# The second MLP of a mixer kernel: 768 tokens by slabs, then two blocks of 768 whose first layer takes Strassen's seven products

## The chip, the cores and the metric

The kernel runs on one core of a Trainium2 chip. The metric is the device time of one execution in microseconds. A core has TensorE (matmuls into PSUM, eight banks of 128 x 2 KB), VectorE, ScalarE and GpSimd, each with its own instruction queue worked in order, SBUF as working memory, and DMA engines that the queues of SyncE (SP) and GpSimd (POOL) start here.

## The reference

Three stages follow one another; the change is in the last. `x` there is 4 x 576 tokens of 512 values, so 2304 tokens, 18 tiles of 128.

```python
X = np.fft.fft(x, axis=1); X = np.fft.fft(X, axis=2)
u = x + np.real(X)
un = (u - mean(u)) / sqrt(var(u) + 1e-06)          # over the 512 values
out = u + np.maximum(un @ w_ch1, 0.0) @ w_ch2      # 512x2048, 2048x512
```

Ahead of it stand random-feature attention and a first mixer MLP (tokens, then channels 512-1536-512). The second MLP's weights come as float64 and are used to more than fp32r's precision: a value is split into a high and a low part, and each product is high x high + high x low + low x high, three matmuls.

## The kernel before, in words

All matmuls of the MLPs are fp32r, 128 x 128 weights against up to 512 columns. `widen` (line 253) turns a 1 MB slab of 64-bit weights on VectorE (seven steps) and ScalarE (one) into high and low parts in the buffers `stg`, `cvy`, `cvo` (two of each, pool `cv`), and `slab` (line 334) stores it to HBM as `kept`; that is done in the background of the attention and of the first MLP.

The **second MLP** has 16 slabs of 128 hidden units, and walks the tokens in five blocks: four of 512, one of 256 (lines 1164 to 1171). For each block and slab `up` (line 689) does 12 matmuls (4 slices of the input x 3 products) into a PSUM bank `H`; `relu` (line 776) lets ScalarE write the high part `hh` and VectorE the low part `hl`; `down` (line 1124) adds 3 products for each token tile into four banks `A`, one per tile. `mlp` (line 783) runs `up` of a slab ahead of `down` of the slab before, so TensorE always has a slab's work between a bank's last matmul and its reader. Blocks go through the slabs forwards and backwards in turn (`turns`), and `refill` (line 644) loads slabs from `kept` on SP's queue into up to nine 1 MB buffers (`wa`, `wb`, and the four of `cv` once widening is over), evicting what is used latest, so a part of the slabs stays from one block to the next.

Between the matmuls stands **side work**, a list with a cost for each item in us. `Side.step(budget)` (line 207) is called once per slab, adds the budget to a credit of at most 4.0, and emits items of `lead` as long as the credit pays for them; a `None` in the list ends the step. Instructions are emitted in this order on each engine (`manual_schedule`). `dft(b)` (line 862) makes the spectrum of one batch entry (VectorE sums `even0` to `odd3`, matmuls `stage1e`, `stage1o`, `stage2`, VectorE again in `plus`, `minus`, `nat`), `norm(c)` (line 1069) the statistics and `un`, the normalized rows of block c. `ff_split` (line 1111) turns `un` by TensorE transposes (bank `S`, two of them) into the operand `u`, high and low parts, at the end of the block before.

PSUM: two banks `H`, four `A`, two `S`. The lines that the prediction's steps touch are those named here, and in the trace line 696 is the first layer's matmul, 1132 the second layer's, 779 and 780 the two halves of the relu, 665 the load of a slab, 1116 the transposes.

Of the kernel before, what the change touches and what calls it, by code (L numbers as in the profile page):

```python
# [9 lines left out]
F32 = mybir.dt.float32  # L10
F32R = mybir.dt.float32r
I32 = mybir.dt.int32
# [23 lines left out]
SLOT0_US, SLOT1_US, SLOT_US, FIRST_US, SHORT_US, CH_US, FF_US, SAVED_US = 1.2, 0.45, 1.2, 3.9, 1.2, 3.7, 3.7, 4.0  # L36
# [77 lines left out]
def layout(q, k, v, omega, moe_w_tok1, moe_w_tok2, moe_w_ch1, moe_w_ch2, moe2_w_ch1, moe2_w_ch2):  # L114
# [26 lines left out]
    def slabs(a, b, n):  # L141
        a = a[COL].reshape(4, 128, n, 128).transpose(2, 1, 0, 3).reshape(n, 128, 512)
        b = b[:, COL].reshape(n, 128, 512)
        return words(np.concatenate([a, b], axis=2))

# [8 lines left out]
        "wch": slabs(moe_w_ch1, moe_w_ch2, NCH),  # L154
        "wff": slabs(moe2_w_ch1, moe2_w_ch2, NFF),
# [79 lines left out]

@with_exitstack
def mix_kernel(ctx: ExitStack, tc: tile.TileContext, qt, kt, va, om, w1, w2, wch, wff, t1, t2, out):
# [15 lines left out]
    def widen(src, n, done):  # L253
# [54 lines left out]

        f = n / 1024
        return (load, lambda: (done(st), busy.remove(k))), [  # L310
# [23 lines left out]
    def slab(ff, j):  # L334
        def store(st):
            kept[ff, j] = dram.tile([128, 2, 1024], F32, name="kept")
            side.queue.dma_start(out=kept[ff, j], in_=st["o"].bitcast(F32))
            whole.add((ff, j))
        return widen((wff if ff else wch)[j].bitcast(I32), 1024, store)
# [195 lines left out]
    def tok_weights():  # L535
# [17 lines left out]
        def chunk(w, lo, n, done):  # L553
            return widen(w.bitcast(I32)[:, 2 * lo:2 * lo + 2 * n], n, lambda st: done(st, lo))
# [63 lines left out]
    mlp0 = {}  # L618

    def enter_mlp():  # L620

        pl.close()
        for name, n in (("ub", 1), ("wa", 1)):
            mlp0[name] = ctx.enter_context(tc.tile_pool(name=name, bufs=n, reuse_waits="tile"))
        u = mlp0["u"] = operand()
        slots.extend((mlp0["wa"], f"wa{i}") for i in range(2))

        def begin():
            mlp0["hb"] = up(weights(*seq[0]), *u, ch_cols(0))

        early.extend([refill] + [lambda k=k: ch_split(0, u, [k]) for k in range(4)])
        early.extend([refill, begin])
# [5 lines left out]
    seq = [(False, j) for c in range(NBLK) for j in turns(NCH, c)]  # L638
    seq += [(True, j) for c in range(B + 1) for j in turns(NFF, c)]
    slots = []  # L640
    here = {}
    at = [0]

    def refill(need=None):

        if (True, NFF - 1) in whole and len(here) + len(slots) < 8:
            slots.extend((cv, tag) for tag in ("stg0", "stg1", "cvo0", "cvo1"))
        for q in range(at[0], len(seq)):
            s = seq[q]
            if s in here:  # L650
                continue
            if s == need:
                side.until(lambda: s in whole)
            if s not in whole:
                return
            if slots:
                slot = slots.pop(0)
            else:
                after = {h: seq.index(h, at[0]) if h in seq[at[0]:] else len(seq) for h in here}
                h = max(after, key=after.get)  # L660
                if after[h] <= q:
                    return
                slot = here.pop(h)[0]
            t = slot[0].tile([128, 2, 1024], F32R, tag=slot[1], name="w")
            sync.dma_start(out=t.bitcast(F32), in_=kept[s])
            here[s] = slot, t

    def weights(ff, j):
        if (ff, j) not in here:
            refill((ff, j))  # L670
        return here[ff, j][1]
# [17 lines left out]
    def up(wt, uh, ul, n):  # L689

        hi, lo = halves(wt, 0)
        hb = bank("H")
        c = 0
        for kk in range(4):
            for a, u in ((hi, uh), (hi, ul), (lo, uh)):
# [497 lines left out]
```

## Time and profile before

| | us |
|---|---|
| three runs | 964.81, 966.81, 967.01 |
| median | 966.81 |
| span of the profiled execution (first to last instruction) | 962.7 |
| TensorE busy | 944.0 (98%) |
| VectorE busy | 556.3 (58%) |
| ScalarE busy | 273.2 (28%) |
| GpSimd busy | 106.9 (11%) |

The profile is of one execution, which has no time of its own in the list of runs: its span is 4.1 us under their median. Times in rows are us from the span's start unless marked ns. Matmuls are pipelined, so a matmul's own duration overlaps its neighbour's; what one costs is read from the starts of many.

### The profile page before, as it was taken

To read this page: it belongs to the slowest core of one execution; us is meant where nothing else is said; L and a number is where in the kernel's file an instruction comes from. 1 tells how busy PE (TensorE), PEld (TensorE's weight loads), DVE (VectorE), ACT (ScalarE), POOL (GpSimd) and SP (SyncE) were. 2 spreads that over 40 slices of the span, in tenths; PEclk is the share of its full clock that TensorE was granted. 3 is DMA by queue.
4 is the path that set the end of the run, shared out by engine and by line. 5 is a ranking of instruction groups with operands and counts; after the bars stand their busy time and mean duration, and the time that the engine had idled before them with its cause. 6 is when DMAs were issued, how large, how long until landed. Compare 5 with 4: busy or idle time off the path is not lost.

```text
span 962.7 us, 13202 instructions
## 1 busy us (share of the span) xinstructions
PE 944.0 (98%) x5248; PEld 820.6 (85%) x5248; DVE 556.3 (58%) x1100; ACT 273.2 (28%) x613; POOL 106.9 (11%) x102
## 2 busy tenths in 40 slices
PE   7999998999999999999999999999999999999998
PEld 7999898888889988888888888888888888888897
DVE  5997989986776777766767532154345434411211
ACT  5876765742122212211312111111111111210111
POOL 3443333321110011000000000000000000000000
PEclk9999999999999999999999999999999999999999
DMA  8764454388898495373376672034103410351080
GB/s 269 232 201 163 148 215 180 126 307 321 344 392 334 158 353 182 146 251 126 132 262 219 225 305 82 0 131 176 44 1 131 175 45 1 115 191 44 24 324 25
DMA packets 33261, 170.80 MB, mean 177 GB/s; under 512 B 3632, under 2 KB 4272, under 8 KB 15664
## 3 DMA queue, kind: packets, MB, share of 16 engines
q1 hardware_dynamic: 27152, 126.78, 36.9%
q0 software_dynamic: 5904, 43.06, 11.8%
q8 instruction: 41, 0.67, 0.3%
q14 instruction: 20, 0.16, 0.1%
q10 hardware_dynamic: 144, 0.13, 0.0%
HBM read 132.08 MB, written 34.08 MB: 173 GB/s over the span
## 4 chain that ended last, share of the span: by engine, by line
PE 88%; DVE 10%; ACT 1%; issue 1%; DMA 0%; DVEq 0%; ACTq 0%
PE H L696 36%; PE A L1132 20%; PE A L819 15%; PE A L413 3%; PE A L574 2%; PE H L447 2%; DVE mx L427 2%; PE N L489 2%; PE S L997 1%; DVE cvo L298 1%; DVE x L505 1%; PE S L1010 1%; PE S L587 1%; PE S L1116 1%; DVE cvo L306 1%; PE S L574 1%
## 5 line engine op out<-in xcount | busy, mean ns | idle before, releaser
L696 PE MATMUL H<-uh,w 128*128 128x512 f32 (+1 forms) x1120 | 341.0, 371 | 1.5 <-ACT x L528 1.5
L780 DVE SCALAR_TENSOR_TENSOR hl<-H,hh 128x512 fp32r<-128x512 f32 (+1 forms) x140 | 89.2, 637 | 257.5 <-ACT hh L779 257.1
L696 PEld LDWEIGHTS H<-uh,w 128*128 128x128 f32 x1120 | 205.0, 189 | 36.5 <-ACT x L528 1.7
L779 ACT ACTIVATE hh<-H 128x512 fp32r<-128x512 f32 (+1 forms) x140 | 77.8, 555 | 506.3 <-PE H L696 504.1
L696 PE MATMUL H<-ul,w 128*128 128x512 f32 (+1 forms) x560 | 206.3, 368 | 0.0
L1132 PE MATMUL A<-w,hh 128*128 128x512 f32 x576 | 146.9, 391 | 0.0
L1132 PEld LDWEIGHTS A<-w,hh 128*128 128x128 f32 x576 | 106.6, 188 | 21.0
L696 PEld LDWEIGHTS H<-ul,w 128*128 128x128 f32 x560 | 105.6, 189 | 16.7
L819 PE MATMUL A<-hh,w 128*128 128x512 f32 (+1 forms) x480 | 108.7, 369 | 0.0
L819 PEld LDWEIGHTS A<-hh,w 128*128 128x128 f32 x480 | 84.2, 188 | 15.0
L1132 PE MATMUL A<-w,hl 128*128 128x512 f32 x288 | 80.6, 390 | 0.0
L431 ACT ACTIVATE f<-A,mx 128x128 f32<-128x128 f32 x200 | 57.5, 388 | 29.6 <-DVE mx L427 25.3
L1132 PEld LDWEIGHTS A<-w,hl 128*128 128x128 f32 x288 | 54.1, 188 | 11.4
L819 PE MATMUL A<-hl,w 128*128 128x512 f32 (+1 forms) x240 | 59.2, 368 | 0.0
L427 DVE TENSOR_REDUCE mx<-A 128x4 f32<-128x512 f32 x71 | 48.3, 682 | 4.3 <-PE A L413 2.9
L819 PEld LDWEIGHTS A<-hl,w 128*128 128x128 f32 x240 | 42.6, 188 | 7.6
L298 DVE SCALAR_TENSOR_TENSOR cvo<-cvo,stg 128x1024 f32<-128x1024 int32 (+2 forms) x32 | 41.0, 1283 | 0.0
L447 PE MATMUL H<-v,f 128*128 128x65 f32 x320 | 40.0, 270 | 0.0
L447 PEld LDWEIGHTS H<-v,f 128*128 128x128 f32 x320 | 39.1, 192 | 0.2 <-DVE kvs L452 0.2
L294 DVE SCALAR_TENSOR_TENSOR cvo<-cvy,cvo 128x1024 int32<-128x1024 int32 (+2 forms) x32 | 38.6, 1207 | 0.4
L306 DVE SCALAR_TENSOR_TENSOR cvo<-cvo,cvy 128x1024 fp32r<-128x1024 f32 (+2 forms) x32 | 38.8, 1212 | 0.0
L282 ACT ACTIVATE cvy<-cvy 128x1024 f32<-128x1024 f32 (+2 forms) x32 | 32.6, 1019 | 14.3 <-DVE cvy L275 14.3
(187 smaller groups left out, 1185.6 us busy)
## 6 DMA issues: line engine op xcount, KB each, us to landing
w<-kept SPq DMA_DIRECT2D x80, 1024.0 KB, 5.1
kept<-cvo POOLq DMA_DIRECT2D x21, 1024.0 KB, 6.3
stg<-in_wff_dram POOLq DMA_DIRECT2D x16, 1024.0 KB, 6.1
stg<-in_wch_dram SPq DMA_DIRECT2D x9, 1024.0 KB, 6.2
kept<-cvo SPq DMA_DIRECT2D x7, 1024.0 KB, 5.2
v<-in_va_dram SPq DMA_DIRECT2D x20, 260.0 KB, 4.0
ks<-in_kt_dram SPq DMA_DIRECT2D x18, 256.0 KB, 3.7
qs<-in_qt_dram SPq DMA_DIRECT2D x18, 256.0 KB, 2.7
```

The costliest lines, as they stand in the source:

```text
L282: act.mul(out=st["y"], in_=st["y"], mul=2.0 ** -112)
L294: dve.scalar_tensor_tensor(out=st["h"], in0=st["y"].bitcast(I32), scalar=-0x80000000, in1=st["h"], op0=ALU.bitwise_and, op1=ALU.bitwise_or)
L298: dve.scalar_tensor_tensor(out=st["l"].bitcast(F32), in0=st["l"], scalar=2.0 ** 32, in1=st["lw"].bitcast(U32), op0=ALU.mult, op1=ALU.add)
L306: dve.scalar_tensor_tensor(out=st["o"][:, 1, 0:n], in0=st["l"].bitcast(F32), scalar=2.0 ** -52, in1=st["y"], op0=ALU.mult, op1=ALU.mult)
L427: dve.tensor_reduce(out=mx, in_=p4, axis=AX.X, op=ALU.max, negate=True)
L431: act.activation(out=f[:, hh], in_=p4[:, hh], func=AF.Exp, bias=mx[:, hh])
L447: pe.matmul(out=kvp[b, g][:, hh * 65:hh * 65 + 65], lhsT=ft["k", i, g][:, hh, :], rhs=src["v", i, int(off > 0)][:, 4 * g + hh, :], start=( ...
L696: pe.matmul(out=hb[:, 0:n], lhsT=a[:, kk * 128:kk * 128 + 128], rhs=u[:, kk, 0:n], start=(c == 0), stop=(c == 11))
L779: act.activation(out=hh, in_=hb[:, 0:n], func=AF.Relu)
L780: dve.scalar_tensor_tensor(out=hl, in0=hb[:, 0:n], scalar=0.0, in1=hh, op0=ALU.max, op1=ALU.subtract)
L819: pe.matmul(out=acc[i][:, 0:cols], lhsT=a[:, cs], rhs=v, start=(j == 0 and c_ == 0), stop=(j == NCH - 1 and c_ == 2))
L1132: pe.matmul(out=acc[t], lhsT=a[:, t * 128:t * 128 + 128], rhs=w, start=(j == 0 and c_ == 0), stop=(j == NFF - 1 and c_ == 2))
```

## The change

The 18 token tiles are divided anew (`ROWS`). Tiles 0 to 3 (512 tokens) and 4 to 5 (256) keep the old way, slab by slab, as blocks 0 and 1. Tiles 6 to 11 and 12 to 17 are two *paired blocks* of 768 tokens each. There the 16 slabs are taken as 8 pairs of 256 hidden units; the first layer of a pair is a product of a 2 x 2 matrix of weight quarters (128 hidden units x 256 inputs each) with a 2 x 2 matrix of operand quarters (256 inputs x 384 tokens), and takes seven products (Winograd's form of Strassen's method: P1 to P7) where eight would be the plain way. Each product is 6 matmuls of 384 columns (2 slices x 3 products of parts). The sums that join products are done on VectorE (`u2`, `vv`, `held`, `c21`) from banks `X` and `Y`, the two `H` banks.

A paired block goes in two passes (`paired_block`). In the first, per pair, the seven products give hidden values of all 768 tokens; those of the first 384 tokens go through the relu and, one pair later, through the second layer (18 matmuls, `todo`, spread between the products in lots of 4, 5, 4 and 5); those of the other 384 wait unrectified in `held`. The second pass does the second layer of `held`, slab by slab backwards, 9 matmuls a slab, while the next block's operands are made (`prepare_ff`).

The four sums of weight quarters (P3, P5, P6, P7) are made once per pair: `sum_pair` on GpSimd (one sum of 1024 columns, four of 256, and the low part of 1024), with a copy on ScalarE, in blocks 0 and 1, and are stored to HBM beside the quarters. The sums of operand quarters are made with the transposes: for the first paired block partly in block 1 (`prepare_early`) and, for P3, P7 and P4, inside its first pair (`prepare_late`), which turns 18 of the 24 tiles again; for the second in the first's second pass.

Weights of the paired blocks are loaded in pieces of 512 KB (two products' quarters, or a slab's second layer) into six buffers (`ffw`); nothing is kept from one block to the next. Blocks 0 and 1 have six buffers of 1 MB (`wd` is new, those of `cv` are gone). `refill` has become a class `Slots` with the same rule of eviction; the last two slabs are bound to three of the buffers. Steps of side work come twice per slab in blocks 0 and 1, at 1.3 and 0.65, and four times a pair in the paired blocks, at 1.5; CH_US goes from 3.7 to 4.0.

```diff
-SLOT0_US, SLOT1_US, SLOT_US, FIRST_US, SHORT_US, CH_US, FF_US, SAVED_US = 1.2, 0.45, 1.2, 3.9, 1.2, 3.7, 3.7, 4.0
+SLOT0_US, SLOT1_US, SLOT_US, FIRST_US, SHORT_US, CH_US, FF_US, S_US, SAVED_US = 1.2, 0.45, 1.2, 3.9, 1.2, 4.0, 2.6, 1.5, 4.0
+NP = NFF // 2
+HALF = 384
+RT = HALF // 128
+PLAIN = [range(0, 4), range(4, 6)]
+PAIRED = [range(6, 12), range(12, 18)]
+ROWS = PLAIN + PAIRED
+P1, P2, P4, P6, P3, P7, P5 = 0, 1, 3, 4, 5, 6, 7
+PIECES = [(P1, P6), (P2, P5), (P3, P7), (P4,)]
...
+    def keep(queue, to, t):
+        for a in range(2):
+            queue.dma_start(out=to[:, :, a], in_=t.bitcast(F32)[:, a].rearrange("p (c n) -> p c n", c=4))
+    def first(p):
+        def store(st, free):
+            kept[1, p] = dram.tile([128, 8, 2, 256], F32, name="kept1")
+            keep(side.queue, kept[1, p][:, 0:4], st["o"])
+            whole.add((1, p))
+            free()
+        return widen(wff[2 * p].bitcast(I32), 1024, store)
...
+    mix.allow = lambda q, slot: q < len(mix.seq) - 2 or slot[1] in ("wa0", "wa1", "wd")
...
+    def sum_pair(p):
+        k = p % 2
+        w = mix.get((1, p))
+        y = cv.tile([128, 1024], F32, tag=f"cvy{k}", name="cvy")
+        v = y.rearrange("p (c n) -> p c n", c=4)
+        pool.tensor_tensor(out=v, in0=w[:, :, 0], in1=w[:, :, 1], op=ALU.add)
+        pool.tensor_tensor(out=v[:, 3], in0=v[:, 2], in1=v[:, 3], op=ALU.add)
+        pool.tensor_tensor(out=v[:, 2], in0=v[:, 0], in1=v[:, 2], op=ALU.subtract)
+        pool.tensor_tensor(out=v[:, 0], in0=v[:, 3], in1=v[:, 0], op=ALU.subtract)
+        pool.tensor_tensor(out=v[:, 1], in0=v[:, 1], in1=v[:, 0], op=ALU.subtract)
+        so = cv.tile([128, 2, 1024], F32R, tag=f"cvo{k}", name="so")
+        def high():
+            act.copy(out=so[:, 0], in_=y)
+            side.later(low, 1)
+        def low():
+            pool.tensor_tensor(out=so[:, 1], in0=y, in1=so[:, 0], op=ALU.subtract)
+            side.later(store, 3)
+        def store():
+            keep(sync, kept[1, p][:, 4:8], so)
+            whole.add((3, p))
+        side.later(high, 4)
...
+            if c == 0 and n % 2 and n < NFF - 1:
+                sum_pair(x[0])
...
+    def prepare_late(q):
+        xa, xb, t2 = held[NP - 1][:, 0], held[NP - 1][:, 1], temps()[2 + q]
+        def b12():
+            act.copy(out=xb, in_=turned(0, q, 1))
+        def b22():
+            pb = turned(0, q + 2, 1)
+            dve.tensor_tensor(out=xb, in0=pb, in1=xb, op=ALU.subtract)
+            parts_of(P3, q, pb)
+        def b21():
+            pb = turned(0, q + 2, 0)
+            dve.tensor_tensor(out=xa, in0=pb, in1=t2, op=ALU.subtract)
+            parts_of(P7, q, xb)
+            parts_of(P4, q, xa)
+        return [b12, b22, b21]
...
-    for c in range(B + 1):
-        if c in (1, 2):
-            side.lead += dft(1 + c)
-        if c < B:
-            side.lead += norm(c + 1)
-        v = operand() if c < B else None
-        ff_block(c, u, ff_prepare(c + 1, v) if c < B else [], FF_US)
-        u = v
+    side.lead += norm(1) + dft(2)
+    v = operand()
+    ff_block(0, u, ff_prepare(1, v), FF_US)()
+    side.lead += norm(2) + [None, (0.0, begin_ff)] + prepare_early(0) + prepare_early(1)
+    put = ff_block(1, v, [], FF_US / 2)
...
+    side.drain()
+    pm.close()
+    fp = ctx.enter_context(tc.tile_pool(name="fp", bufs=1, reuse_waits="tile"))
+    ff = {}
+    flow = []
+    due = []
...
+    def fetch_ff(x, pl_, tag):
+        k, p_, i = x
+        if k == 2:
+            t = pl_.tile([128, 2, 512], F32R, tag=tag, name="w2t")
+            sync.dma_start(out=t.bitcast(F32), in_=kept[2, p_][:, :, i * 512:i * 512 + 512])
+            return t
+        ids = PIECES[i]
+        t = pl_.tile([128, 2, 2, 256], F32R, tag=tag, name="w1t")
+        step = ids[1] - ids[0] if len(ids) > 1 else 1
+        sync.dma_start(out=t[:, 0:len(ids)].bitcast(F32), in_=kept[1, p_][:, ids[0]:ids[-1] + 1:step])
+        return t
...
+    def product(to, w, i, start):
+        uh, ul = operands(i)
+        n = 0
+        for q in range(2):
+            cs = slice(q * 128, q * 128 + 128)
+            for a, v in ((0, uh), (0, ul), (1, uh)):
+                pe.matmul(out=to, lhsT=w[:, a, cs], rhs=v[:, q], start=(start and n == 0), stop=(n == 5),
+                          skip_group_check=True)
+                n += 1
...
+    def paired_block(c, todo, uses, after):
+        s1, u2, vv, c21 = temps()
+        acc = [None] * RT
+        def pace():
+            if c or p_:
+                side.step(S_US)
+        for p_ in range(NP):
+            X, Y = (bank("H")[:, 0:HALF] for _ in range(2))
+            h = hbuf[4 * (p_ % 2):4 * (p_ % 2) + 4]
+            w = ffw.get((1, p_, 0))
+            product(X, w[:, 0], P1, True)
+            act.copy(out=s1, in_=X)
+            product(Y, w[:, 1], P6, True)
+            dve.tensor_tensor(out=u2, in0=Y, in1=s1, op=ALU.add)
+            ffw.used()
+            pace()
+            run(todo, 4)
+            w = ffw.get((1, p_, 1))
+            product(X, w[:, 0], P2, False)
+            relu_parts(h[0:2], X)
+            product(Y, w[:, 1], P5, True)
+            dve.tensor_tensor(out=vv, in0=Y, in1=u2, op=ALU.add)
+            pace()
+            run(todo, 5)
+            ffw.used(1 + uses)
+            w = ffw.get((1, p_, 2))
+            product(Y, w[:, 0], P3, False)
+            dve.tensor_tensor(out=held[p_][:, 0], in0=Y, in1=u2, op=ALU.add)
+            product(X, w[:, 1], P7, True)
+            dve.tensor_tensor(out=held[p_][:, 1], in0=X, in1=vv, op=ALU.add)
+            ffw.used()
+            pace()
+            run(todo, 4)
+            w = ffw.get((1, p_, 3))
+            product(X, w[:, 0], P4, False)
+            dve.tensor_tensor(out=c21, in0=X, in1=u2, op=ALU.add)
+            relu_parts(h[2:4], c21)
+            pace()
+            run(todo)
+            ffw.used(1 + uses)
+            if after:
+                after()
+            after, uses = None, 1
+            if p_ == 0:
+                acc = [bank("A") for _ in range(RT)]
+            for s_ in range(2):
+                todo += downs(acc, h[2 * s_:2 * s_ + 2], (2, p_, s_), p_ + s_ == 0, p_ + s_ == NP)
...
+        for n, x in enumerate(slabs):
+            if n == 1 and steps:
+                side.until(lambda: (len(PLAIN) + c + 1, 2 * RT - 1) in uns, side.lead)
+            if n and steps:
+                steps.pop(0)()
+            if n + 2 < len(slabs):
+                hs[n + 2] = part(n + 2)
+            mats = downs(acc, hs.pop(n), (2, *x), n == 0, n == len(slabs) - 1)
+            if n < len(slabs) - 2:
+                run(mats)
+                ffw.used()
+                side.step(S_US)
+            else:
+                left += mats
+        return left, 1, lambda: finish(c, 1, acc)
...
+    carry = prepare_late(0) + prepare_late(1), 0, None
+    for c in range(len(PAIRED)):
+        if c == 0:
+            side.lead += dft(3) + norm(3)
+        carry = paired_block(c, *carry)
+    run(carry[0])
+    ffw.used(2)
+    carry[2]()
```

## Rows read from the trace of the kernel before

**Rows 1.** The page: busy time of engines (1), chain that ended last by engine (4).

```profile
PE 944.0 (98%) x5248; PEld 820.6 (85%) x5248; DVE 556.3 (58%) x1100; ACT 273.2 (28%) x613; POOL 106.9 (11%) x102
...
PE 88%; DVE 10%; ACT 1%; issue 1%; DMA 0%; DVEq 0%; ACTq 0%
```

**Rows 2.** Windows: stretch, length, busy time by engine, granted clock, DMA share, GB/s.

```profile
0.00:100.00 100.00, 92.70 (x740) 89.58 (x740) 78.61 (x163) 71.37 (x194) 38.82 (x36) 1.00 0.67 217
...
700.00:800.00 100.00, 100.00 (x492) 84.41 (x491) 45.01 (x106) 15.53 (x31) 0.00 (x0) 1.00 0.23 85
```

**Rows 3.** Chain in order of time, end of the fourth and start of the fifth block.

```profile
901.63 2.72 PE A L1132 x12
904.35 2.72 PE H L696 x12
907.51 2.75 PE A L1132 x12
...
917.70 1.43 PE H L696 x12
```

**Rows 4.** Timeline of TensorE, matmuls of 288 columns: six from the first row on.

```profile
211.12 0.42 PE L587 MATMUL S<-w2hl,h1h 128*128 128x288 f32 x2
...
211.91 0.39 PE L696 MATMUL H<-uh,w 128*128 128x512 f32 x1
```

**Rows 5.** Groups by line and shape, pieces of 384 columns: busy, mean ns | idle.

```profile
L686 DVE TENSOR_TENSOR ul<-x,uh 128x384 fp32r<-128x384 f32 x4 | 2.2, 554 | 0.0
...
L685 ACT CAST uh<-x 128x384 fp32r<-128x384 f32 x4 | 2.1, 513 | 0.0
```

**Rows 6.** Timeline of one slab: last matmul of its first layer, then the relu.

```profile
605.14 0.39 PE L696 MATMUL H<-uh,w 128*128 128x512 f32 x1
...
605.57 0.60 ACT L779 ACTIVATE hh<-H 128x512 fp32r<-128x512 f32 x1 [4.84 <-PE H L696]
606.20 0.69 DVE L780 SCALAR_TENSOR_TENSOR hl<-H,hh 128x512 fp32r<-128x512 f32 x1 [4.75 <-ACT hh L779]
```

**Rows 7.** Timeline of VectorE: newton and un; even1 and even2 of a dft.

```profile
481.25 0.17 DVE L1092 RECIPROCAL y<-y 128x4 f32<-128x4 f32 x1
...
482.24 1.92 DVE L1101 TENSOR_SCALAR un<-U,mv,y 128x512 f32<-128x512 f32 x4
...
732.77 0.44 DVE L886 TENSOR_TENSOR sp<-fo 1x289 f32<-1x289 f32 x1
...
734.55 0.67 DVE L780 SCALAR_TENSOR_TENSOR hl<-H,hh 128x512 fp32r<-128x512 f32 x1
735.16 0.44 DVE L893 TENSOR_TENSOR fv<-fo 128x289 f32<-128x289 f32 x1
...
736.48 0.61 DVE L904 TENSOR_TENSOR fo<-fv 128x432 f32<-128x432 f32 x1
```

**Rows 8.** Groups by line and shape: GpSimd's subtractions, VectorE's at 640 columns.

```profile
L516 POOL TENSOR_TENSOR xl<-x,xh 128x512 fp32r<-128x512 f32 x18 | 28.3, 1570 | 29.7 <-ACT xh L515 25.9 <-issue 3.8
...
L401 POOL TENSOR_TENSOR kl<-ks,kh 128x512 fp32r<-128x512 f32 x17 | 22.9, 1349 | 80.9 <-ACT kh L400 63.9 <-PE H L447 8.3 <-DVE kh L398 5.2
...
L298 DVE SCALAR_TENSOR_TENSOR cvo<-cvo,stg 128x640 f32<-128x640 int32 x2 | 1.6, 814 | 0.0
```

**Rows 9.** Timeline of VectorE and GpSimd side by side.

```profile
47.42 1.29 POOL L401 TENSOR_TENSOR kl<-ks,kh 128x512 fp32r<-128x512 f32 x1 [2.55 <-ACT kh L400]
47.80 1.53 DVE L298 SCALAR_TENSOR_TENSOR cvo<-cvo,stg 128x576 f32<-128x576 int32 x1
```

**Rows 10.** Windows as in rows 2, a stretch of the first MLP.

```profile
280.00:310.00 30.00, 30.00 (x221) 28.62 (x220) 19.36 (x33) 6.70 (x15) 2.13 (x4) 1.00 0.98 383
```

**Rows 11.** DMA view of the first 50 us: GB/s in 40 slices; queue: packets, MB, share.

```profile
GB/s 0 56 365 396 348 252 357 140 366 336 352 361 388 392 304 133 74 166 358 37 0 0 0 159 323 383 418 168 229 211 278 389 361 319 113 393 377 222 220 301
...
q1 hardware_dynamic: 5784, 12.36, 78.3%
```

More of the change, by code (lines that the diff above doesn't have):

```diff
@@ L639, in mix_kernel @@
[L639 to L671, printed above, removed]
+    def fetch(x, pl_, tag):
+        if x in PAIR1:
+            t = pl_.tile([128, 4, 2, 256], F32R, tag=tag, name="w")
+            sync.dma_start(out=t.bitcast(F32), in_=kept[x][:, 0:4])
+        else:
+            t = pl_.tile([128, 2, 1024], F32R, tag=tag, name="w")
+            sync.dma_start(out=t.bitcast(F32), in_=kept[x])
+        return t
+    def wait_whole(x):
+        side.until(lambda: x in whole)
@@ L761, in mix_kernel @@
     projection()
-    side.rest += weave(tok_weights() + [slab(False, j) for j in range(NCH)] + [slab(True, j) for j in range(NFF)])
+    side.rest += weave(tok_weights() + [slab(j) for j in range(NCH)]
+                       + [w(p_) for p_ in range(NP) for w in (first, second)])
     attention()
@@ L818, in down @@
                     cs = slice(i * 128, i * 128 + 128)
-                    pe.matmul(out=acc[i][:, 0:cols], lhsT=a[:, cs], rhs=v, start=(j == 0 and c_ == 0),
-                              stop=(j == NCH - 1 and c_ == 2))
-        mlp(False, at_, NCH, u, cols, down, budget, prepare)
+                    pe.matmul(out=acc[i][:, 0:cols], lhsT=a[:, cs], rhs=v, start=(n == 0 and c_ == 0),
+                              stop=(n == NCH - 1 and c_ == 2))
+            mix.used()
+        mlp(turns(NCH, at_), ch_first, u, cols, down, budget, prepare)
         for i in range(4):
@@ L1148, in mix_kernel, with temps @@
+    def temps():
+        return [tmp[k][:, i] for k in range(2) for i in range(2)]
     tables()
@@ new lines, in mix_kernel @@
+    hbuf = [big[i][:, 4 * HALF:5 * HALF] for i in (P1, P6, P2, P5, P3, P7, P4)]
+    hbuf.append(h8)
+    held += [fp.tile([128, 2, HALF], F32, name=f"t2_{p_}") for p_ in range(5, NP)]
+    put()
+    def product(to, w, i, start):
[7 more added lines that the diff above has]
+                n += 1
@@ new lines, in relu_parts, with downs, one @@
+    def relu_parts(h, src):
+        act.activation(out=h[0], in_=src, func=AF.Relu)
+        dve.scalar_tensor_tensor(out=h[1], in0=src, scalar=0.0, in1=h[0], op0=ALU.max, op1=ALU.subtract)
+    def downs(acc, h, x, begins, ends):
+        def one(t, n):
+            w = ffw.get(x)
+            pe.matmul(out=acc[t], lhsT=h[n // 2][:, t * 128:t * 128 + 128], rhs=w[:, n % 2], start=(begins and n == 0),
+                      stop=(ends and n == 2))
+        todo = [(t, n) for t in range(RT) for n in range(3)] if begins or ends else \
+               [(t, n) for n in range(3) for t in range(RT)]
+        return [lambda x=x: one(*x) for x in todo]
```

325 lines of the change are left out of this document (248 added, 77 removed).

## Prediction

> **What bounds the kernel now.** I read the page's busy shares and its chain first, then the chain in order of time through the second MLP, then single instructions. TensorE is busy for 98% of the span and holds 88% of the chain; VectorE has 10% of it, ScalarE 1% [rows 1]. In a 100 us stretch of the second MLP TensorE shows no idle time at all and VectorE is busy for 45 us [rows 2]. The chain in order of time is there one string of first-layer (line 696) and second-layer (line 1132) matmuls [rows 3]. So in the stage that changes, time is the number of matmuls times what one costs, plus whatever wait the change puts in.
>
> A slab of a 512-token block takes 2.72 us for its 12 first-layer matmuls and 2.72 us for its 12 second-layer ones: 226.7 ns each [rows 3], at a granted clock of 1.00, the 2.4 GHz level [rows 2]. In the last, 256-token block 12 first-layer matmuls take 1.43 us, 119.2 ns each [rows 3]. Six matmuls of 288 columns take 211.91 - 211.12 = 0.79 us, 131.7 ns each [rows 4]. The line through 256 and 512 is 0.42 ns per column with 11.7 ns fixed; it gives 132.6 ns at 288, so it holds between its ends. At 384 columns, a size the trace does not show, it gives **173 ns**. Bounds: 170 ns (three quarters of 226.7) and 226.7 ns (no saving for the narrower operand); I take the line, because a third size lies on it.
>
> **The change, part by part.** *First layer of 1536 tokens.* Removed: three 512-token blocks, 3 x 16 slabs x 12 = 576 matmuls, 576 x 226.7 = 130.6 us. Added: 2 blocks x 8 pairs x 7 products x 6 = 672 matmuls of 384 columns, 672 x 173 = 116.3 us. Net **-14.3 us**. The second layer is 18 tiles x 16 slabs x 3 = 864 matmuls on both sides, and the 512- and the 256-token block keep their cost (16 x 5.44 and 16 x 2.82 us); the latter only moves forward.
>
> *Transposes.* Four of them lengthen the gap from 904.35 + 2.72 to 907.51, 0.44 us, 0.11 us each [rows 3]. The first paired block turns 24 tiles early and 18 of them a second time; the second turns 24. Against 72 before that is 18 more: **+2.0 us**.
>
> *The first pair of the first paired block.* Here no second-layer matmuls lie between the products; the six steps of the late preparation do. VectorE's and ScalarE's pieces are 384 wide: 0.55 us and 0.51 us at the same width [rows 5], on VectorE about 0.47 from start to start. The hand-over from matmul to ScalarE to VectorE to matmul is short: the matmul that starts at 605.14 is read at 605.57, and VectorE starts 0.03 us after ScalarE ends [rows 6]. In program order VectorE does 16 pieces from u2 to c21 (7.5 us, beginning 2.2 us into the pair), stands four times behind a ScalarE piece that it needs (1.9 us), and c21 needs the last product, which itself starts only after VectorE has read X (about 1.9 us more with hand-overs). So the next pair begins at about 13.5 us, where TensorE's own work is 42 x 0.173 + 18 x 0.11 = 9.3: **+4.2 us**. From below, only the two turns of X that nothing covers, 2 x 0.75 = 1.5; from above 6, if every ScalarE piece is waited for.
>
> *A pair in the steady state* is 42 x 0.173 + 18 x 0.2267 = 11.35 us. VectorE's own seven pieces are 3.9 us, ScalarE's three 1.5. P2 to P4 and the next P1 each find four or five second-layer matmuls (0.91 or 1.13 us) ahead of them, against 0.75 us for the read that they wait for: cost 0, cover 0.2 to 0.4 us. That cover is gone wherever side work stands ahead of the read. In the first paired block dft(3) and norm(3) run at 1.5 us of credit per step, four steps a pair. Counted through by the costs in the source, two steps are too long. One holds even1 and even2, 1.78 + 1.32 us in the instance at 732.77 and 735.16 [rows 7]; behind held1 (0.7 us after P7) it lets X go 4.4 us after P7, where TensorE wants it after 0.91 + 1.04 + 1.13 = 3.1: 1.3 us. One holds newton and six un, 1.0 + 6 x 0.48 us by the instance at 481.25 and 482.24 [rows 7]; behind vv it lets held1 end 5.6 us after P5, wanted after 4.1: 1.5 us. Together **+2.8 us**; bounds 0 and 8 (each of the other long steps losing 0.5 us). The second paired block has no side work.
>
> *At nothing.* The sums of quarters: GpSimd took 1.35 to 1.57 us for a 128x512 subtraction [rows 8]; a pair's sums are 2 x 1024 and 4 x 256 columns, 2 x 2.8 + 4 x 0.7 = 8.4 us, in a pair's 10.9 us, and first wanted over 40 us later; the ScalarE copy, 1.1 us as an estimate from 0.60 at half the width, sits in the 4.8 us that ScalarE idles before each relu [rows 6]. VectorE beside GpSimd is stretched: at 47.80 a 576-column operation took 1.53 us beside GpSimd's at 47.42, where 640 columns take 0.81 [rows 8, 9]. In the 512-token block VectorE's dft steps meet the sums; hl ends at 606.89 [rows 6] and is first used after a slab's 5.44 us less 1.5 and 8 matmuls of 0.227, 5.7 us later, so 0.7 us an operation costs nothing. The Trainium skill ("SBUF — State Buffer", The single rule) calls the pair of ports that VectorE's two-input operations share with GpSimd an exclusive lock for the whole instruction; by it a burst could also sit out the 5.8 us of five sums and a stall of some 1 us appear, which I leave to the range. *Queues.* SP is in order: each load waits for the buffer that TensorE frees, and the stores of sums wait for GpSimd's low, issued some 8 us earlier. GpSimd's queue now stores each first-layer slab in two parts of 1 KB runs; what stands behind them there is the next load, two chunks ahead of its use. *The 256-token block* has six weight buffers where it had nine: ten slabs, 10.5 MB, come in within some 34 us, 310 GB/s; 383 GB/s were moved at 280 to 310 us [rows 10]. Cost 0, bound 3. The lead queue fits: about 34 us of items into 39 us of credit, then 16 into 19.5; if it does not, what is left is drained before the paired blocks, bound 4.
>
> **Sum:** -14.3 + 2.0 + 4.2 + 2.8 = **-5.3 us** on the profiled execution, 962.7 to 957.4 us of span. The median of the three runs, 966.81, is 4.1 us above that span, time around it that stays: **961.5 us**. A difference under 0.3%, 2.9 us, can't be told from none.
>
> **Rivals.** (a) *The waits hide.* If the steps fall where VectorE is idle and the first pair loses only its two turns, -14.3 + 2.0 + 1.5 = -10.8: 956.0 us. For it: VectorE is busy for under half of this stage [rows 2]; against: program order. (b) *The waits double.* The cover of 0.2 to 0.4 us is thin, and a late read delays every later one in the pair: 8.4 + 5.6 in place of 4.2 + 2.8 gives +1.7, 968.5 us: no change. (c) *The narrow matmul does not pay*, so that the seven products save nothing: at 200 ns the 672 cost 134.4 us, the sum is +12.8, 979.6 us. The point is 181 ns, from which the whole gain is gone. Against it: three sizes on one line.
>
> (d) *Slower: the transfers become the bound.* Nothing of the weights stays in SBUF in the paired blocks. One block reads 8 x 2.75 MiB and then 8 MiB, both 62.9 MB, in 247 us: 255 GB/s, in pieces of 512 KB with mostly 2 KB runs, from six buffers. The nearest row is the first 50 us, where loads of 256 KB in 2 KB runs dominate: 12.36 MB took 78.3% of the engines' time, 316 GB/s at full share [rows 11]. Below 255 GB/s this decides; at the 217 GB/s that the first 100 us averaged [rows 2], with engines partly idle, it would be 290 us, 43 us more, some 1004 us. The Trainium skill ("DMA: Bandwidth & Descriptors", Bandwidth) wants transfers of 1 MiB or more and gives a fixed 2 us plus the bytes at 436 GB/s; 512 KB one at a time would by it move at an estimated 164 GB/s. The trace speaks against transfers one at a time: several are in flight, and 1.25 us slices of those 50 us reach 418 GB/s [rows 11].
>
> **How the numbers follow.** Forecast as summed, from -3 to -9: 0.50. (a) 0.12. (b) 0.22. (c) 0.07. (d) 0.09. Faster by over 0.3%: 0.50 + 0.12; same: 0.22; slower: 0.16. The range runs from 954 (case a with 2 us off the matmul at 170 ns) to 973 (case b with the bound of the lead queue); it leaves out most of (c) and (d).
>
> **What would show it.** Right: first-layer matmuls of 384 columns 173 ns apart; TensorE waiting for VectorE in the first pair of the first paired block by 3 to 6 us, and there in two more places; none in the second paired block, whose pairs take 11.35 us and whose second pass 16 x 2.04 us. Wrong: gaps ahead of P1, P3 or the second-layer matmuls put down to DMA, pairs longer than 11.6 us in the second paired block, or GpSimd's sums ahead of a product.

## The result, and the profile after

The changed kernel takes 979.35 us, median of four runs (974.76 to 980.28), against 966.24 us in the four runs of the kernel before beside it: a ratio of 1.0128, 95% interval 1.0103 to 1.0153. It is slower by over 1%, and outside the predicted range. Executions of one kernel differ: in six of the fourteen profiles of this study (the changed kernel's is one) the granted clock is also 0.83 or 0.91 at 160 to 180 us, in the others 1.00, in code that is the same, so differences of medians below some 2 us are weak. The profiled execution took 978.46 us with a span of 976.7 us, 14.0 us more than the 962.7 us of before, where the sum said 5.3 us less. So 19.3 us are to be found.

The page of the changed kernel (busy time; chain by engine), to be read against [rows 1]:

```profile
PE 944.5 (97%) x5362; PEld 836.1 (86%) x5362; DVE 626.9 (64%) x1222; ACT 300.7 (31%) x676; POOL 182.6 (19%) x158
...
PE 83%; DVE 13%; ACT 2%; issue 1%; DMA 0%; DVEq 0%; ACTq 0%
```

TensorE is as busy as before, in a longer span, and five hundredths of the chain have gone from it, most to VectorE: TensorE waits for VectorE in places where it did not. Where, the windows tell (columns as in [rows 2]; the column behind POOL is the granted clock):

```profile
534.00:560.00 26.00, 23.88 (x120) 20.08 (x119) 14.04 (x40) 3.10 (x7) 0.00 (x0) 0.93 0.18 66
...
580.00:600.00 20.00, 17.74 (x80) 14.85 (x79) 12.03 (x20) 3.32 (x6) 11.25 (x8) 0.91 0.56 178
600.00:620.00 20.00, 16.88 (x79) 13.93 (x78) 9.88 (x18) 3.61 (x7) 10.76 (x9) 0.91 0.55 187
...
842.00:934.00 92.00, 92.00 (x481) 85.10 (x480) 31.49 (x57) 11.46 (x23) 0.00 (x0) 1.00 0.74 247
```

In the 512-token block, from 534 us on, TensorE stands idle for 2 to 3 us in each of the three stretches shown, and the granted clock there is 0.91 to 0.93. In the second paired block it is busy without a gap at 1.00, while 247 GB/s of weights come in. The chain in order of time (start, us, what, number of matmuls), where [rows 3] answers:

```profile
534.74 2.74 PE H L772 x12
...
541.75 4.34 PE H L772 x12
...
866.93 2.10 PE H L1450 x12
869.04 0.93 PE A L1463 x4
...
878.43 1.58 PE H L1450 x9
...
934.78 36.55 PE A L1463 x161
```

Line 772 is the first layer, 1450 Strassen's products, 1463 their second layer. Twelve matmuls of 384 columns take 2.10 us, 175 ns each; a pair takes 878.43 - 866.93 = 11.50 us; the second pass of the last block goes at 36.55 / 161 = 227 ns. So the narrow matmuls pay as forecast. But the second slab of the 512-token block takes 4.34 us for the twelve matmuls that the first did in 2.74: it follows a wait of 1.87 us, and part of it runs at the 1.2 GHz level (granted clock 0.50 from 543 to 546 us).

The waits of TensorE in the 512-token block (bank, line, waited for: us, times, longest):

```profile
PE S L1047 <- DVE fo L974: 2.3, 1, 2.3
PE S L1086 <- DVE U L1081: 1.9, 1, 1.9
PE S L1056 <- DVE fo L1018: 1.9, 1, 1.9
PE S L1057 <- DVE fo L974: 1.2, 1, 1.2
PE S L1086 <- DVE gath L1121: 0.2, 1, 0.2
```

Lines 1046 to 1057 are the first matmuls of the transform, 1086 its transposes. All five wait for VectorE's side work, none for the relu. VectorE (953, 955 and the relu's second half, 857) and GpSimd (1222, a 1024-column subtraction of the sums) just before the first of them, in the timeline:

```profile
567.70 0.69 DVE L857 SCALAR_TENSOR_TENSOR hl<-H,hh 128x512 fp32r<-128x512 f32 x1 [2.90 <-ACT hh L856]
568.31 0.75 DVE L953 TENSOR_TENSOR fo<-x 128x574 f32<-128x574 f32 x1
569.10 2.24 DVE L955 COPY fo<-x 128x4 f32<-128x4 f32 x1
571.25 0.74 DVE L953 TENSOR_TENSOR fv<-x 128x574 f32<-128x574 f32 x1
572.03 2.24 DVE L955 COPY fv<-x 128x4 f32<-128x4 f32 x1
...
568.69 2.63 POOL L1222 TENSOR_TENSOR so<-cvy,so 128x1024 fp32r<-128x1024 f32 x1 [34.99 <-ACT so L1218]
571.39 2.86 POOL L1210 TENSOR_TENSOR cvy<-w 128x1024 f32<-128x1024 f32 x1
```

A copy of four columns takes 2.24 us, twice, each until a GpSimd operation of 1024 columns ends (571.32 and 574.25 us). The earliest of the long waits is another matter: GpSimd does nothing from 534 to 560 us, where the wait of 1.9 us at line 1086 lies.

By stages, against the sum: the 512-token block takes 117.1 us (534.6 to 651.7) where 103.4 were due, 13.7 more. (Due: the 94.96 us of before's first block, 9.3 us for the transform that now lies in it too, less 0.9 for eight transposes; a transform is what before's second and third block, 97.95 and 98.42 us, hold over 16 slabs of 5.44 us and 16 transposes, 9.2 and 9.6 us.) The five waits are 7.5 of the 13.7 us. The clock is some 5.4 more, an estimate from the windows: 0.07 of 26 us and 0.09 of 20 us twice. The 256-token block takes 49.6 for some 47.8 (16 slabs of 2.82 us and 24 transposes). From the first product to the last matmul it is 271.4 us where the sum made some 268. The start is 0.6 us late (534.58 for 533.98). So over two thirds of the error lie in the one block that the prediction kept at its cost.

### The profile page after: what moved, and what is told of

Its sections match the earlier page's. It is cut to its first block, busy times and chain, and to the rows that moved or that the text cites. A ratio compares the mean times of both kernels' runs of the same rounds, so it can differ in the third digit from the quotient of the medians.

```text
span 976.7 us, 14107 instructions
## 1 busy us (share of the span) xinstructions
PE 944.5 (97%) x5362; PEld 836.1 (86%) x5362; DVE 626.9 (64%) x1222; ACT 300.7 (31%) x676; POOL 182.6 (19%) x158
## 4 chain that ended last, share of the span: by engine, by line
PE 83%; DVE 13%; ACT 2%; issue 1%; DMA 0%; DVEq 0%; ACTq 0%
PE H L772 21%; PE A L894 15%; PE A L1463 13%; PE H L1450 11%; PE A L1255 5%; PE A L502 3%; PE A L663 2%; PE N L578 2%; PE H L536 2%; DVE mx L516 2%; PE S L1073 1%; DVE cvo L360 1%; PE S L1086 1%; PE S L676 1%; DVE x L594 1%
## 5 line engine op out<-in xcount | busy, mean ns | idle before, releaser
L772 PE MATMUL H<-uh,w 128*128 128x512 f32 (+1 forms) x736 | 216.2, 362 | 1.5 <-ACT x L617 1.5
L772 PEld LDWEIGHTS H<-uh,w 128*128 128x128 f32 x736 | 134.1, 190 | 22.1 <-ACT x L617 1.7
L772 PE MATMUL H<-ul,w 128*128 128x512 f32 (+1 forms) x368 | 132.5, 360 | 0.0
L1463 PE MATMUL A<-w2t,b 128*128 128x512 f32 x384 | 100.8, 394 | 0.0
L1450 PE MATMUL H<-b,w1t 128*128 128x384 f32 x480 | 92.0, 337 | 1.7 <-DVE t L1510 0.9
L1450 PEld LDWEIGHTS H<-b,w1t 128*128 128x128 f32 x480 | 84.0, 188 | 7.1 <-DVE t L1510 3.4
L1463 PEld LDWEIGHTS A<-w2t,b 128*128 128x128 f32 x384 | 70.7, 188 | 11.6
L772 PEld LDWEIGHTS H<-ul,w 128*128 128x128 f32 x368 | 70.1, 190 | 9.9
L1255 PE MATMUL A<-w,hh 128*128 128x512 f32 x192 | 51.8, 402 | 0.0
L1255 PEld LDWEIGHTS A<-w,hh 128*128 128x128 f32 x192 | 35.3, 193 | 6.2
```

Of the source, the lines that this page charges most:

```text
L772: pe.matmul(out=hb[:, 0:n], lhsT=w(a, kk), rhs=u[:, kk, 0:n], start=(c == 0), stop=(c == 11))
L1255: pe.matmul(out=acc[t], lhsT=a[:, t * 128:t * 128 + 128], rhs=w, start=(n == 0 and c_ == 0), stop=(n == NFF - 1 and c_ == 2))
L1450: pe.matmul(out=to, lhsT=w[:, a, cs], rhs=v[:, q], start=(start and n == 0), stop=(n == 5), skip_group_check=True)
L1463: pe.matmul(out=acc[t], lhsT=h[n // 2][:, t * 128:t * 128 + 128], rhs=w[:, n % 2], start=(begins and n == 0), stop=(ends and n == 2))
```

## The experiments

Theory A: GpSimd's sums hold VectorE up beside them, TensorE waits at the transform's matmuls, and each long wait is followed by matmuls at half the clock. Theory B: the block now takes its side work in half steps, twice a slab, so TensorE meets VectorE's results after half a slab in place of a whole one. The two paired stages play no part in this, so I give for each run the time of the 512- and the 256-token block together (start of the first first-layer matmul to that of the first product, in the profiled execution) beside the median. Some 151.2 us were due for the two; the changed kernel took 166.7.

**No sums.** `sum_pair` without its GpSimd operations:

```diff
-        pool.tensor_tensor(out=v, in0=w[:, :, 0], in1=w[:, :, 1], op=ALU.add)
...
+        act.copy(out=so[:, 0], in_=w[:, :, 0])
...
-            pool.tensor_tensor(out=so[:, 1], in0=y, in1=so[:, 0], op=ALU.subtract)
+            act.copy(out=so[:, 1], in_=so[:, 0])
```

> Leaves out the sums and differences of weight quarters (ScalarE copies two quarters' worth of words in their place, so the paired blocks multiply by weights that are not Strassen's), in number and size of transfers all as in the changed kernel. The first block of the second MLP, from its first first-layer matmul to that of the next block, took 117.1 us in the changed kernel, and 103.4 us was worked out for it without any wait. Theory A (GpSimd's sums stretch the VectorE operations beside them, TensorE waits at the transform's matmuls, and runs at half its clock behind each wait): the block takes 104 to 107 us, the kernel 966 to 970 us. Theory B (the half-slab steps do it: TensorE meets VectorE's results half a slab after they were started): the block stays at 114 to 117 us and the kernel at 976 to 980 us. Theory C (the clock alone, by chance of the execution): single times as before between 974 and 981 us.

971.58 us, 7.8 less; the first block 108.3 us, 8.8 less, but not the 104 to 107 of theory A. The wait of 1.9 us at line 1086 is still there, with the clock at 0.93 behind it and no GpSimd operation in that stretch. Theory A explains most, and not that. (In the second block, 52.7 us, a wait of 2.9 us is new: ScalarE's casts wait for the transfer of the last words out of the same buffer.)

**Full steps.**

```diff
-        mlp(steps, first_of, u, 128 * len(tiles), down, budget, prepare, True)
+        mlp(steps, first_of, u, 128 * len(tiles), down, budget, prepare, c > 0)
...
-    ff_block(0, u, ff_prepare(1, v), FF_US)()
+    ff_block(0, u, ff_prepare(1, v), 3.7)()
```

The delays in `sum_pair` go from 4 and 3 steps to 2 and 1, as a step is now twice as long.

> The sums stay; the first block takes its side work once a slab with 3.7 us, as the kernel before did, and not twice a slab with 1.3 us. Theory A: VectorE is held up by the sums as much as before but has twice the time before TensorE meets its results, so a part is won: the block takes 108 to 114 us, and VectorE's copies beside the 1024-column sums still take over 2 us each; the kernel 970 to 976 us. Theory B: no wait is left, the block takes 103 to 106 us, the kernel 965 to 969 us. Theory C: no change, 974 to 981 us.

967.52 us, two blocks 158.0 us. The first block is 101.2, since part of the transform has moved into the second, 56.8; only the two together can be compared. Theory B's time, but not its mechanism alone: VectorE is still held up, as the waits and the timeline of VectorE show:

```profile
PE H L772 <- DMA w<-kept: 1.8, 1, 1.8
PE S L1047 <- DVE fo L974: 1.0, 1, 1.0
PE S L1057 <- DVE fo L974: 0.7, 1, 0.7
```

```profile
581.82 2.67 DVE L963 TENSOR_TENSOR sp<-fo 1x289 f32<-1x289 f32 x1
...
585.56 2.55 DVE L969 TENSOR_TENSOR fv<-fo 128x289 f32<-128x289 f32 x1
```

Both take 0.44 us without the sums. Two such hold-ups, 4.3 us, now cost 1.0 us of waiting. The longest wait left is one for a weight transfer, 1.8 us until 671 us, and the clock of 665 to 675 us is 0.88; no operation of GpSimd or VectorE ends that wait. The profiled execution took 971.88 us, 4.4 above the median, so its 158.0 us for the two blocks is on the high side.

**Both.** The two edits together.

> Both edits at once: no sums on GpSimd (left out, as in the run without sums), and full steps. Theories A and B both expect a block of 103 to 105 us and a kernel of 963 to 967 us. If the block still takes over 110 us, neither of the two is the cause, and theory C or a third one stands.

964.93 us, ratio 0.9994 (0.9985 to 1.0004); two blocks 153.0 us. The two causes hold all but 1.8 us of the 15.5.

**Sums cut up.** Six operations become twelve of 256 columns:

```diff
-        pool.tensor_tensor(out=v, in0=w[:, :, 0], in1=w[:, :, 1], op=ALU.add)
+        for i in range(4):
+            pool.tensor_tensor(out=v[:, i], in0=w[:, i, 0], in1=w[:, i, 1], op=ALU.add)
...
-            pool.tensor_tensor(out=so[:, 1], in0=y, in1=so[:, 0], op=ALU.subtract)
+            for i in range(4):
+                cs = slice(256 * i, 256 * i + 256)
+                pool.tensor_tensor(out=so[:, 1, cs], in0=y[:, cs], in1=so[:, 0, cs], op=ALU.subtract)
```

> The sums stay on GpSimd, but its two 1024-column operations of a pair are cut into four of 256 columns each; half steps as in the changed kernel. Theory A, with each VectorE operation held up by the GpSimd operation that it meets, until that one ends: no VectorE copy of the transform takes over 1.2 us where some took 2.4, and the block falls by 3 to 8 us, to 109 to 114 us; kernel 971 to 976 us. If VectorE is instead slowed for as long as GpSimd is at work at all, nothing is won (115 to 118 us, 977 to 981 us). Theory B: nothing is won.

970.03 us, two blocks 158.4 us, the first one 108.9. The same work on GpSimd, and 8.2 of the 8.8 us that leaving it out gave, though GpSimd is busy for longer (65 us of 534 to 700 us, for 55). The copy of four columns in this run, and in a run without sums (below), in the groups by line and shape (busy, mean ns):

```profile
L955 DVE COPY fo<-x 128x4 f32<-128x4 f32 x1 | 0.6, 591 | 0.0
```

```profile
L857 DVE SCALAR_TENSOR_TENSOR hl<-H,hh 128x512 fp32r<-128x512 f32 x16 | 11.0, 690 | 52.0 <-ACT hh L856 52.0
...
L955 DVE COPY fo<-x 128x4 f32<-128x4 f32 x1 | 0.2, 171 | 0.0
```

0.17 us alone, 0.59 beside 256 columns, 2.24 beside 1024: a hold-up ends when the GpSimd operation that was met ends. What decides is how long one operation is, not how much GpSimd does.

**Full steps and cut sums.** Both edits.

> Full steps and the 1024-column sums cut into four, together. The two first blocks together took 166.7 us in the changed kernel, 158.0 with full steps alone, 158.4 with the cut sums alone, 153.0 with full steps and no sums. Theory A+B (two causes that add up: the steps cost some 8 us, the sums some 5, of which cutting them takes back most): 153 to 156 us in the two blocks, the kernel 963 to 966 us, the same as the kernel before or a little faster. If cutting only helps where the steps are short, it stays at 158 us and 967 to 968 us.

966.77 us (963.04 to 972.0), ratio 1.0011 (0.9994 to 1.0027), two blocks 152.6 us in a profiled execution of 964.29. The stage does what was expected; the median is above the range, with runs far apart, and can't be told from the kernel before.

**Doubled breaks.** Half steps and long sums stay; every break in the list of items counts twice:

```diff
     side.lead += norm(1) + dft(2)
+    side.lead = [y for x in side.lead for y in ([x, x] if x is None else [x])]
```

> The changed kernel with half steps of 1.3 us kept and the sums as they are, but with every break in the transform's list of items doubled, so that a result of VectorE is again met by TensorE a whole slab after it was started. Theory B1 (the distance between an item and the next after a break is what the half steps took away): most of the 8 us comes back, the two first blocks take 157 to 161 us, the kernel 966 to 971 us, and the wait of 1.9 us of the transposes early in the block is gone. Theory B2 (it is the dose: 1.3 us at a time spread over two places, whose items lie ahead of the relu's second half each time): no change, 164 to 168 us and 974 to 981 us.

977.93 us, two blocks 165.9: the times that B2 gave, but not its picture. The early wait of 1.9 us at line 1086 is gone and the clock of 534 to 560 us is 1.00, as B1 said, but waits of 2.6, 2.5 and 2.0 us stand at the transform's first matmuls, and one at the second layer, for the relu's second half:

```profile
PE A L1255 <- DVE hl L857: 1.0, 1, 1.0
```

VectorE before them:

```profile
577.01 0.16 DVE L1170 TENSOR_TENSOR z<-y 128x2 f32<-128x2 f32 x1
577.21 2.40 DVE L1171 TENSOR_TENSOR z<-z,ve 128x2 f32<-128x2 f32 x1
579.63 0.17 DVE L1172 TENSOR_SCALAR z<-z 128x2 f32<-128x2 f32 x1
579.84 2.24 DVE L1173 TENSOR_TENSOR y<-y,z 128x2 f32<-128x2 f32 x1
...
589.02 2.03 DVE L969 TENSOR_TENSOR fv<-fo 128x289 f32<-128x289 f32 x1
590.97 2.64 DVE L970 TENSOR_TENSOR fv<-fo 128x289 f32<-128x289 f32 x1
```

```profile
580.00:600.00 20.00, 14.43 (x62) 11.38 (x61) 18.70 (x24) 3.09 (x5) 14.37 (x11) 0.90 0.83 289
```

Operations of two columns take up to 2.4 us. GpSimd's last subtraction of one pair and the first addition of the next stand one behind the other in its queue, so they come as two long operations in a row, and four hold-ups in 16 us are some 8 us that even a whole slab does not cover. VectorE is busy for 18.7 of 20 us.

**Doubled breaks, no sums; doubled breaks, cut sums.**

> Half steps, doubled breaks, and no sums on GpSimd (left out, as in the earlier runs without sums). With doubled breaks and the sums the two first blocks took 165.9 us and the kernel 977.9 us; without the sums and with single breaks 160.9 us and 971.6 us; without the sums and with full steps 153.0 us and 964.9 us. Theory B1 (distance): without GpSimd beside, the doubled breaks do what full steps do, 153 to 156 us, 965 to 968 us, and what spoilt them before was the sums alone. Theory B2 (the dose twice a slab): still 159 to 162 us, 970 to 973 us.

> Half steps, doubled breaks, and the sums kept on GpSimd, with their two 1024-column operations cut into four. If the length of one GpSimd operation is what made VectorE too late even with a whole slab between (theory A), this falls by 8 us or more against 977.9 us, to 964 to 969 us, and no wait over 1.5 us is left beside the sums. If it is the sum of GpSimd's work, it stays above 974 us.

963.5 us (ratio 0.9971, 0.9959 to 0.9983) and 963.17 us (0.9970, 0.9958 to 0.9982); two blocks 151.3 and 152.4 us. Half steps as such cost nothing. What they took away is the distance between an item and the matmul that needs it. (A doubled break also leaves the half step behind it empty, and its credit goes into the next, so the doses grow too; that the distance is what counts is argued from the changed kernel's waits, which were all for the items' results.) The 151.3 us is, within 0.1 us, what was due for the two blocks without a wait. With cut sums these are all the waits in the two blocks:

```profile
PE S L1047 <- DVE fo L974: 0.7, 1, 0.7
PE S L1086 <- ACT le L1126: 0.4, 1, 0.4
```

The two blocks in one table:

| two blocks, us | no sums | 256 columns | 1024 columns |
|---|---|---|---|
| half steps | 160.9 | 158.4 | 166.7 (the change) |
| half steps, doubled breaks | 151.3 | 152.4 | 165.9 |
| full steps | 153.0 | 152.6 | 158.0 |

Each cell is one profiled execution, within 1 us of the median of its kernel's runs, except two: full steps with 1024 columns (4.4 us above its median) and with 256 (2.5 us below). By medians the long sums cost 7.8 us with half steps, 14.4 with doubled breaks and 2.6 with full steps (967.52 less 964.93).

**A wait filled.** On the kernel without sums, 16 transposes ahead of the four that wait at line 1086:

```diff
+        def more(r):
+            if (b, r) == (1, 0):
+                pb = bank("H")
+                for c in range(16):
+                    pe.transpose(pb[:, c % 4 * 128:c % 4 * 128 + 128], x[:, c % 4, 0:256:2], ident)
```

> On the kernel without the sums (971.6 us), whose only wait over 1 us early in the first block is one of 1.87 us by four transposes, with a granted clock of 0.93 in the 26 us from 534 on. Sixteen more transposes, which nothing reads, go ahead of those four, so that TensorE works for about 1.8 us where it stood. If the wait itself brings the clock down, the clock of that stretch is 1.00 and the kernel takes 1.4 to 2.0 us less, 969.6 to 970.2 us. If the clock falls there for another reason (the switch to another kind of matmul, the transposes), it stays at 0.93 and the time is the same or up to 2 us more.

970.38 us, 1.2 less than without the filling, a little short of the 1.4 expected at least and by itself weak; in the profiled executions the first block takes 105.9 us in place of 108.3, of which 0.6 is a wait at line 1046 that is gone too. The windows of 534 to 560 us, first of the kernel without sums, then with the wait filled:

```profile
534.00:560.00 26.00, 23.88 (x120) 20.21 (x119) 13.57 (x39) 4.15 (x8) 0.00 (x0) 0.93 0.18 60
```

```profile
534.00:560.00 26.00, 25.76 (x143) 22.23 (x142) 14.00 (x40) 4.32 (x9) 0.00 (x0) 1.00 0.23 79
```

TensorE does work that nothing needs, and the block is shorter, because the clock stays at 2.4 GHz. Here the wait itself brings it down, and the price of the second half is about that of the first: 1.6 us (4.34 less 2.74) behind a wait of 1.87. But not every wait does it. In the 256-token block of the same run TensorE waits still longer, until 664.34 us, and the clock stays at 1.00:

```profile
PE S L1294 <- DVE tmp L1346: 2.4, 1, 2.4
```

```profile
660.00:680.00 20.00, 17.61 (x119) 16.03 (x118) 7.57 (x16) 5.77 (x14) 0.00 (x0) 1.00 1.02 415
```

**The sums in the kernel before.** The same six operations for each two slabs, results unused, in its second block:

```diff
+            if c == 1:
+                extra(j, wt)
```

> The kernel before, with GpSimd making the same sums (six operations for each two weight slabs, eight times, results not used) in the second block of the second MLP, beside the transform of the third batch, with full steps as they are. The prediction's step, that the sums cost nothing there since the relu's second half has 5.7 us in hand: 0 us, within 1 us of the kernel before. Theory A (the sums stretch the transform's VectorE work, and TensorE waits for that, not for the relu): 3 to 6 us slower, with waits of the transform's matmuls for VectorE that the kernel before does not have there, and copies of 128x4 that take over 2 us.

967.03 us, ratio 1.0003 (0.9994 to 1.0012), and no wait of TensorE in the whole second MLP. I expected 3 to 6 us, a miss. (GpSimd's queue runs ahead: four of the eight pairs are done at 580 to 613 us, in the block before.) The hold-ups are there, in the timeline of VectorE:

```profile
654.87 2.67 DVE L936 TENSOR_TENSOR fv<-fo 128x288 f32<-128x288 f32 x1
...
660.99 0.68 DVE L780 SCALAR_TENSOR_TENSOR hl<-H,hh 128x512 fp32r<-128x512 f32 x1
662.24 0.88 DVE L956 TENSOR_TENSOR sh<-S,sh 128x258 fp32r<-128x258 f32 x2 [0.57 <-ACT sh L955]
```

The dose that ended at 656.9 us without sums ends at 661.1, and the next operation that follows a matmul starts at 662.24 in place of 662.00, which is as late as the whole stretch is in this run. The matmul that reads the dose's result:

```profile
661.17 0.38 PE L980 MATMUL S<-t_sb,fo 128*128 128x129 f32 x2
```

It starts 0.1 us behind the dose's end. Full steps hide 4 us of hold-ups here, and that is all the cover the old steps had: that this run shows no cost is by 0.1 us.

**Smaller doses in the paired blocks.** `S_US` 1.2 in place of 1.5, on full steps with cut sums and then on doubled breaks with cut sums.

> As full steps with cut sums, and in the paired blocks the last transform and norm in doses of 1.2 us a quarter pair in place of 1.5. If the 3.4 us of waits in the rest of the first paired block come from the size of the doses, they fall to 1 to 2 us and the kernel is 1.5 to 2.5 us faster than with full steps and cut sums; if single long items of 1.0 to 1.7 us make them, they stay, and the time is the same within 1 us.

> The correct kernel that was fastest so far (half steps, doubled breaks, sums cut into 256 columns: 963.2 us) with the smaller doses of 1.2 us in the paired blocks. With full steps those shortened the part from the first pair to the last matmul from 271.3 to 269.3 us, and here that part stood at 270.3 us: if the doses do it by themselves, 1 to 2 us are won, 961 to 962.5 us; if the doubled breaks had already taken those waits away, nothing changes, 962.5 to 964 us.

963.28 us (0.9978, 0.9961 to 0.9994) and 962.79 us (0.9967, 0.9952 to 0.9982). From the first product to the last matmul it is 269.3 us for 271.3 in the first case, 269.8 for 270.3 in the second: the doses make part of the waits there. Behind the first pair of the first paired block TensorE waits 2.2 us with full steps and 0.7 with the smaller doses, and 1.8 and 1.0 with doubled breaks. (The 3.4 us expected from the changed kernel counts one wait of the first pair twice; it is 2.5.) In the second case 962.79 us lies where "nothing changes" was put. The doubled breaks, which end ahead of that stage, had already brought it to 270.3: their first pair waits 1.2 us in place of 1.7 at line 1297, a transpose; why, I did not follow. The last kernel is the fastest of the study, 0.33% under the kernel before; the one without the smaller doses is as good within the interval.

## Why the prediction was wrong

*What held.* The matmul of 384 columns: 175 ns where the line of [rows 3, 4] gave 173, so the first layer won about 13.0 us (130.6 less 672 x 175 ns) for 14.3. Rivals (c) and (d) are out: 175 is below the point of 181 ns, and in the second paired block 247 GB/s came in with no wait for a transfer. The first pair took 13.4 us for 13.5 (701.27 us to 714.63, which is six matmuls of P4 behind the start of this row; the other twelve are the next pair's P1 and P6):

```profile
713.58 3.42 PE L1450 MATMUL H<-b,w1t 128*128 128x384 f32 x18 [0.85 <-DVE t L1510]
```

That figure is in part luck: its waits were 2.7 us for 4.2, and TensorE's own work 10.7 for 9.3. The rest of the first paired block waited 2.5 us in three places, for 2.8 in two: 1.0 ahead of P3 and 0.8 ahead of P5 behind side work, which I had put ahead of P4, and 0.7 at a matmul of the transform. So rival (b), waits that double, is out too. A pair in the second block took 11.50 us for 11.35.

*What failed: the step "At nothing".* The sums were put at 0 us because hl, the relu's second half, has 5.7 us in hand. Two things were wrong in it. First, it is the wrong reader. hl itself is not lengthened (0.69 us in the changed kernel and without the sums alike), no wait of the changed kernel's block is for it, and TensorE needs the transform's operands far sooner. Where hl did come late (1.0 us, with doubled breaks) it stood in VectorE's queue behind operations that were. Cover has to be counted to the matmul that reads the held-up operation's result. Second, the duration: 0.7 us for an operation came from one instance beside a GpSimd operation of 512 columns [rows 9], where a 1024-column one costs up to 2.4 us, and several follow in one dose. (That instance, too, fits a hold-up to the end of the GpSimd operation: this came at 48.71 us, 0.6 us before VectorE's ended.) The Trainium skill ("SBUF — State Buffer", Who interferes with whom, the single rule) has the rule that I left to the range: it speaks of a lock for a whole instruction, names copies in a mode that uses both pairs of ports and operations with two inputs in SBUF as those that meet it, and leaves out others with at most one input there. The trace agrees on all three: 0.17 to 2.24 us for a copy, 0.44 to 2.67 us for a two-input operation, and 0.69 us unchanged for hl, whose first input is in PSUM. A stall "of some 1 us" was the forecast; the price in this block was 8 to 9 us with half steps, by the runs without sums and with cut ones.

*What was left out: the half steps.* The diff moves half of the side work to a second place in the slab. I counted its credit, not what it does to the distance between an item and its reader. It costs 6 us by itself (158.4 against 152.4 with cut sums and doubled breaks), and it uncovers the hold-ups. The two do not simply add: by the medians the long sums cost 2.6 us with full steps, 8 with half steps, 14 with doubled breaks, and in the kernel before nothing, by how many hold-ups fall into one dose and how much cover it has.

*What was not in it at all: the clock.* A wait of 1.9 us cost some 3.5 us (1.87, and 1.6 at the half clock), and with the wait filled the clock did not fall. The prediction priced waits at their own length.

*What stays open.* With the causes removed and the smaller doses the change wins 2.8 us, 965.58 to 962.79, where 5.3 were forecast. In the changed kernel the paired blocks take 3.4 us more than the sum made, though their waits are 1.8 us shorter; 15 pairs at 0.15 us are 2.2 of it and TensorE's longer work in the first pair 1.4, and of the rest, some 1.6 us, I have no account. Why full steps bring a wait of 0.6 to 1.8 us for a weight transfer into the second block was not tried, nor why a wait brings the clock down in one place and not in another. That the long sums cost nothing in the kernel before may be due in part to where its doses happen to stand: four of the eight pairs of sums ran in the block before, and the one dose looked at had 0.1 us left.

## What to carry to other kernels

When an idle engine is given work beside a busy one, count the cover of each operation that it can hold up to the matmul that reads that operation's result, and take a hold-up to be as long as the longest single instruction beside it: cutting the helper's long instructions to a quarter won nearly as much as leaving them out. When side work is dealt out in finer steps, keep the distance between producer and reader in time, not in steps. Where the rows show TensorE's clock fall behind waits, price such a wait at up to nearly twice its length: not each of them brings it down.

## What was not expected of the hardware

The granted clock fell behind single waits of 1.87 us (0.93 over 26 us), 1.8 us for a transfer (0.88 over 10 us) and 2.3 us (0.91 over 20 us), whatever they waited for. It did not fall behind every wait of that size: one of 2.40 us left it at 1.00, and of two waits of 1.69 us at the same transposes of the first paired block one was followed by 0.91 over 20 us (full steps, long sums, until 699.07) and the other by 1.00 (full steps, cut sums, until 692.72). Twelve matmuls behind the first wait took 4.34 us in place of 2.74. Where the longest wait was 0.7 us the clock stayed at 1.00 through both blocks. An operation of two columns on VectorE can take 2.40 us for 0.16 when it meets a long GpSimd operation, and GpSimd is held up in its turn: its first 256-column addition took 2.32 us at 574.33 us, for 0.74 elsewhere.
